# Three entries of a schedule moved: early weight loads, a layer's conversion, one group's row gathers

## The chip, the cores and the metric

The kernel runs on one core of a Trainium2 chip. The metric is the device time of one execution in microseconds (us). Before the change the median of three runs is 801.74 us (800.7 to 805.22).

## What is computed

Three layers follow each other, all in float32 (cut from the reference):

```python
# 1. attention, B, H, S, D = 4, 8, 576, 64
scores = q @ k.T / sqrt(D);  cum = cumsum(max(s, 0))
scores = where(causal, -1e9, scores + min(-(cum_i - cum_j), 0))
x = softmax(scores) @ v                      # -> x: 2304 tokens x 512
# 2. mixture of experts: each token goes to one of 8 experts, D 512, F 1024
e = argmax(x @ w_gate);  gate = softmax(x @ w_gate)[e]
x = gate * (max(x @ w1[e], 0) @ w2[e])
# 3. dense layer, 512 -> 768 -> 512
h = max(x @ m1, x @ m2, x @ m3)              # elementwise maximum of three products
out = h @ w_out
```

The weights of layer 3 arrive as 64-bit words and are turned into float32 on the chip (the "conversion" below).

## The kernel before

**Attention.** The 32 heads are worked in 16 pairs, 4 pairs to a batch. A pair loads k, q, v (`nk`, `nq`, `nv`) and its bias rows `bl` (two DMAs of 528 KB, L218). POOL writes the causal mask into `bl` (L269, L274, L280). PE makes scores (L308, L328), DVE adds the bias and takes the row minimum of the negated scores (L314, L335), ACT takes the exponential (L321, and L343 for the last rows, once to a pair), PE transposes the result (L374), ACT and DVE copy it out of PSUM (L416, L414), PE multiplies by v (L426). While a pair is scored, the pair before it is transposed and multiplied. The expert choice of a batch (L488 to L557) runs beside the pairs after it.

**Experts.** Tokens are gathered by expert into groups of up to 336 rows (`gather`, L926, an indirect DMA on POOL's queue; one buffer of three windows to a group, two buffers), transposed on PE (L932), split into a high and a low float32r half on ACT and DVE (L944, L948) and multiplied in three matmuls (L953). Group 0 takes tokens of the first three batches and starts before attention ends; group 1 is the first full group that waits for the last batch.

**Weight ring.** Expert weights come in pieces of 512 KB: `w_load` (L689, an SP DMA into `wr0` to `wr2`, later also `xr0`, `xr1`), `w_hi` (ACT rounds the piece to its high half, listed as L192) and `w_lo` (DVE subtracts, L697). The first three pieces, `n < R0` (L722), belong to group 0 and are handled during attention. They take their times from five numbers in line 80: `w_hi` of piece n at slot `WE1 + WES * n`, that is 80, 126 and 172, and its load `WE0` slots from there.

**Conversion.** `decode` (L764) takes one of 24 chunks of the dense layer's weights through a load on ACT's queue (`dr`, 512 KB, L735), one ACT operation (L739), six DVE operations (L743 to L759) and a store on ACT's queue (L762). Inside a chunk the ACT operation is due `D0` = 5 us after the load and the store `DST` = 13 us after it.

**What sets the order.** Every step is put into one list with a due slot (`at`, L202; a slot is 0.456 us, a pair lasts `IT` = 25 slots). The list is sorted by slot and emitted (`run_events`, L1103), so the slot fixes only where an instruction stands in its own engine's queue. When it runs is decided by semaphores: a slot starts nothing, and an engine takes its instructions strictly in that order. `TX` is the slot at which the attention's buffers are given up, `TM` the planned start of group 1's matmuls, 11.2 us later in plan time, and `TOV` lies near the end of the last group.

Of the kernel before, what the change touches and what calls it, by code (L numbers as in the profile page):

```python
# [12 lines left out]
I32 = mybir.dt.int32  # L13
# [19 lines left out]
NEARLY = 1  # L33
# [38 lines left out]
LD0, SPL, VT = 3, 9, 10  # L72
WLF = 12
ORD = (3, 1, 2, 0)
D0, DST = 5, 13

WRB, R0, R1, XR, XQ = 3, 3, 2, 2, 1
WHI = "A"
WLO = "V"
WE0, WE1, WES, WEL, WEH = -23, 80, 46, 3, "A"  # L80
WHE, WLE = "A", "V"
SLOT = 0.456
ES, TMS = 5.0, 2
# [15 lines left out]
def emit(nc, tc, qt, kt, v, s, wg, w1, w2, m64, out, dbg=None):  # L99
    V, A, G, T, SP = nc.vector, nc.scalar, nc.gpsimd, nc.tensor, nc.sync  # L100
# [101 lines left out]
    def at(slot, fn, *args):  # L202
        heapq.heappush(evq, (slot, next(seqno), fn, args))
# [424 lines left out]
    TX = max(e[0] for e in evq) + 1  # L628
    cap = [c for e, bs, c in GROUPS]
    TM = max(TX + 13, TA + (ES + NEARLY * 21.2) / SLOT) + TMS  # L630

    def atm(us, fn, *args):
        at(TM + us / SLOT, fn, *args)
# [34 lines left out]
    def pt(g, i):  # L668

        x, k = step[g]  # L670
        us = SL[x] / 8 * i + sum(cost[o] for o in STEPS[x][:k]) / 8 + (GAP12 if i >= 4 else 0)
        return S0[x] + us / SLOT

    TOV = pt(NG - 1, 4) + OVT / SLOT
# [89 lines left out]
    def decode(u, src, dst, n):  # L764
        z = {}
        atm(u, dec_load, z, src, n)
        for x, f in ((D0, dec_abs), (D0 + 1, dec_1), (D0 + 2, dec_2), (D0 + 3, dec_3), (D0 + 4, dec_4)):
            atm(u + x, f, z, n)
        atm(u + DST, dec_st, z, dst, n)


    for n in range(24):
        dst = w32 if n < 18 else wo32
        i, x = divmod(n if n < 18 else n - 18, 2)
        decode((TX - TM) * SLOT + 1 + ((TOV - TX) * SLOT - 4 - DST) / 23 * n, m64[n].bitcast(I32), dst[i, :, 512 * x:512 * x + 512], 512)


    gi = cp.tile([P, NG * NWIN], I32, name="gi")
# [124 lines left out]
    XG1 = max(TR2, TA) + 0.2  # L903
# [102 lines left out]
    gfree = [0.0, 0.0]  # L1006
    for x, gs in enumerate(STEPS):

        span = (S0[x] - 1.3 / SLOT) - max(S0[x] - 9 / SLOT, max([last.get("x", -1e9)] + [last.get("xs", -1e9)]) + 0.3 / SLOT,
                                          TX + 7 if x >= NEARLY else -1e9)  # L1010
        if x == 0:
            span = 1.2 / SLOT
        st_ = min(1.7 / SLOT, max(0.3 / SLOT, span / (4 * len(gs))))
        m = 0
        for g in gs:
            L = cost[g]
            t0 = S0[x] - 1.3 / SLOT - st_ * (4 * len(gs) - m)
            gfree.sort()
            if g == 0:
                at(XG0, gather, g)  # L1020
            else:
                at(max(gfree[0] + 0.01, XG1 if x < NEARLY else TX + 0.2, t0 - 60 / SLOT), gather, g)
                gfree[0] = t0 + st_ * 3 + 0.02
            for kk in range(4):
                t = t0 + st_ * kk
                at(t, xtr, g, kk)
                at(t + 0.3 / SLOT, xhi, g, kk)
                if not small(g):
                    at(t + 0.8 / SLOT, xlo, g, kk)
            m += 4  # L1030
            for f in range(8):
                t = pt(g, f // 2) + (f % 2) * L / 16 / SLOT
                at(t, mm1, g, f)
                at(t + (L / 16 + 0.1) / SLOT, h_hi, g, f)
                if not small(g):
                    at(t + (L / 16 + 0.5) / SLOT, h_lo, g, f)
            last["xs" if small(g) else "x"] = t + L / 16 / SLOT
            for d_ in range(4):
                t = pt(g, 4 + d_)
                at(t, mm2, g, d_)  # L1040
                at(t + (L / 8 + 0.1) / SLOT, y_ev, g, d_)
# [208 lines left out]
```

## Time and profile before

| | us |
|---|---|
| median of three runs | 801.74 |
| lowest, highest | 800.7, 805.22 |
| the profiled execution | 801.6 |
| span of its trace (first to last instruction) | 799.9 |

The trace is of the profiled execution: 1.7 us of its time lie outside the span. From 0 to about 223 us attention runs, with group 0's first matmuls in its last part, then the experts until about 489 us, then the dense layer. A share over the whole span mixes these three; what one step costs is read from its own stretch. In the timelines a value in square brackets is the time for which that engine sat idle before the row, and behind the arrow stands what released it. "SPq" and "ACTq" rows are DMA issues; their duration is the issue, not the transfer.

### The profile page before, as it was taken

Reading aid. Unit: us, or ns where it says so; the run is one execution under the profiler, and the core shown is the slowest. Engines: PE = TensorE matmul, PEld = TensorE weight load, DVE = VectorE, ACT = ScalarE, POOL = GpSimd, SP = SyncE. Lnnn points to the kernel's source line nnn. Section 1 sums busy time; section 2 is a strip of 40 time slices with the busy share of each in tenths; the row PEclk is TensorE's granted clock in tenths of the full one; section 3 lists DMA queues with packets and bytes.
Section 4 is the critical chain, followed back from the end, with each engine's and each line's share of the span. In section 5 each row is a group of like instructions: output and inputs, shape, how many; then the busy total and the mean of one; then the engine's idle time right before and its main releaser. Section 6 shows DMA issues by size and latency. Waiting matters only on the chain. (4 is left out here: it accounts for less than half of the span.)

```text
span 799.9 us, 12890 instructions
## 1 busy us (share of the span) xinstructions
PE 763.0 (95%) x4782; PEld 685.6 (86%) x4782; DVE 436.9 (55%) x1142; ACT 335.4 (42%) x771; POOL 110.8 (14%) x226
## 2 busy tenths in 40 slices
PE   7988999999879999999999999999999999999996
PEld 4755666666679988999999999989989899899995
DVE  6655777677668768889888755422312212222120
ACT  5755666666546443455445545221211211212111
POOL 4332233334130110101200000010010000100001
PEclk9999999999999999999999999999999999999999
DMA  6866968767376687877685535100010000100001
GB/s 187 208 163 168 257 156 246 187 174 238 95 273 229 216 292 255 298 255 265 216 256 196 202 131 152 58 27 14 1 40 1 23 18 1 40 1 14 26 1 40
DMA packets 34876, 112.43 MB, mean 141 GB/s; under 512 B 4793, under 2 KB 4875, under 8 KB 32891
## 3 DMA queue, kind: packets, MB, share of 16 engines
q1 hardware_dynamic: 24107, 81.66, 34.3%
q10 hardware_dynamic: 7456, 18.89, 6.8%
q0 software_dynamic: 3248, 11.03, 3.9%
q8 instruction: 39, 0.64, 0.3%
q14 instruction: 26, 0.21, 0.1%
HBM read 94.97 MB, written 16.60 MB: 139 GB/s over the span
## 5 line engine op out<-in xcount | busy, mean ns | idle before, releaser
L1146 DVE TENSOR_TENSOR mA<-ps_a,mA 128x384 f32<-128x384 f32 x72 | 40.2, 558 | 181.4 <-PE ps_a L953 181.4
L953 PE MATMUL ps_a<-yc,wq 128*128 128x384 f32 x720 | 129.1, 339 | 0.0
L953 PEld LDWEIGHTS ps_a<-yc,wq 128*128 128x128 f32 x720 | 127.4, 188 | 0.4
L953 PE MATMUL ps_c<-h,wq 128*128 128x336 f32 (+1 forms) x672 | 106.3, 316 | 3.1 <-ACTq L870 1.5
L953 PEld LDWEIGHTS ps_c<-h,wq 128*128 128x128 f32 x672 | 101.8, 192 | 3.9 <-ACTq L870 1.8
L953 PE MATMUL ps_a<-yc,wm 128*128 128x384 f32 x576 | 103.7, 339 | 0.0
L953 PE MATMUL ps_a<-xT,wq 128*128 128x336 f32 (+1 forms) x648 | 101.0, 313 | 1.9 <-ACT hs L972 1.6
L953 PEld LDWEIGHTS ps_a<-yc,wm 128*128 128x128 f32 x576 | 101.9, 188 | 0.0
L953 PEld LDWEIGHTS ps_a<-xT,wq 128*128 128x128 f32 x648 | 96.5, 188 | 2.6 <-ACT hs L972 1.8
L953 PE MATMUL ps_c<-wm,g 128*128 128x512 f32 x324 | 76.9, 396 | 0.0
L321 ACT ACTIVATE P<-ns,mn 128x512 f32<-128x512 f32 (+3 forms) x128 | 70.7, 559 | 12.8 <-DVE mn L314 12.8
L1150 ACT ACTIVATE g<-mA 128x384 fp32r<-128x384 f32 x36 | 18.9, 526 | 135.7 <-DVE mA L1146 135.7
L953 PEld LDWEIGHTS ps_c<-wm,g 128*128 128x128 f32 x324 | 60.9, 188 | 14.4
L1169 POOL DMA_INDIRECT out<-o,midi x18 | 17.6, 976 | 378.5 <-ACT o L1165 374.4
L314 DVE CUSTOM_DVE_ANT_0 ns<-ps_a,bl 128x512 f32<-128x512 f32 (+3 forms) x128 | 57.3, 488 | 21.3 <-ACT P L321 11.8
L697 DVE TENSOR_TENSOR wq<-wr,wq 128x1024 fp32r<-128x1024 f32 x44 | 53.6, 1221 | 13.5 <-ACT wq L192 13.0
L426 PE MATMUL ps_c<-ptT,nv 128*64 128x320 f32 (+4 forms) x448 | 51.4, 367 | 5.2 <-DVE ptT L414 5.2
L426 PEld LDWEIGHTS ps_c<-ptT,nv 128*64 128x64 f32 x448 | 29.8, 138 | 31.0 <-DVE ptT L414 12.6
L192 ACT ACTIVATE wq<-wr 128x1024 fp32r<-128x1024 f32 x44 | 46.3, 1055 | 22.4 <-DMA wr<-in_w 22.4
L374 PE MATMUL ps_b<-idf,P 128*128 128x128 f32 x320 | 47.4, 287 | 5.5 <-ACT ptT L416 3.9
L308 PE MATMUL ps_a<-nk,nq 64*128 64x512 f32 (+3 forms) x256 | 48.3, 477 | 2.9 <-DVE mn L314 1.7
L374 PEld LDWEIGHTS ps_b<-idf,P 128*128 128x128 f32 x320 | 35.1, 143 | 15.1 <-ACT ptT L416 9.1
(221 smaller groups left out, 955.5 us busy)
## 6 DMA issues: line engine op xcount, KB each, us to landing
wr<-in_w SPq DMA_DIRECT2D x49, 512.0 KB
bl<-cumd SPq DMA_DIRECT2D x30, 528.0 KB
dr<-in_m ACTq DMA_DIRECT2D x24, 512.0 KB
xr<-in_w SPq DMA_DIRECT2D x23, 512.0 KB
nq<-in_qt SPq DMA_DIRECT2D x16, 352.0 KB
nv<-in_v SPq DMA_DIRECT2D x16, 320.0 KB
nk<-in_kt SPq DMA_DIRECT2D x16, 288.0 KB
xd<-xr SPq DMA_DIRECT2D x4, 1152.0 KB
```

Of the source, the lines that this page charges most:

```text
L192: A.activation(o, x, AF.Copy)
L308: T.matmul(d["sp", i, g][:, :w], d["q"][r, 128 * i:128 * i + 128], d["k"][r, :w], start=True, stop=True)
L314: V.tensor_tensor_reduce(out=ns[:, :w], in0=d.pop(("sp", i, g))[:, :w], in1=d["bl"][:, 1024 * g + BOFF[i]:1024 * g + BOFF[i] + w], scale=- ...
L321: A.activation(pp, d.pop(("ns", i, g))[:, :w], AF.Exp, bias=d["mn"][:, c:c + 1], scale=-1.0, accum_out=ssum[b][:, i, h + g:h + g + 1])
L374: T.transpose(pt[:, c:c + 128], (d["P", "t"] if g == "t" else d["P", g, i])[:, k0:k0 + 128], idf)
L426: T.matmul(po[64 * g:64 * g + 64, qa - c0:c1 - c0], d["v"][:, g, j], d["pt"][:, g, POFF[j] + qa - 128 * j:POFF[j] + c1 - 128 * j], start=( ...
L697: (V if eng == "V" else G).tensor_tensor(t[:, 1], raws.pop(key), t[:, 0].bitcast(F32), ALU.subtract)
L953: T.matmul(ps_, w_(zw), x_(zx), start=(first and n == 0), stop=(last and n == 2))
L1146: V.tensor_tensor(m, pm[:, :CH], m, ALU.max)
L1150: A.activation(t[:, 0], h2[c, f, "m"], AF.Copy)
L1169: G.indirect_dma_start(out, bass.IndirectOffsetOnAxis(ap=midi[:, n:n + 1].bitcast(U32), axis=0), h2.pop((c, x, "s")), None)
```

## The change

Three entries of the schedule get other slots; no operation is added or removed.

```diff
-D0, DST = 5, 13
+DS0, D0, DST = -2, 5, 13
...
-WE0, WE1, WES, WEL, WEH = -23, 80, 46, 3, "A"
+WE0, WE1, WES, WEL, WEH = -45, 80, 46, 3, "A"
...
     for n in range(24):
         dst = w32 if n < 18 else wo32
         i, x = divmod(n if n < 18 else n - 18, 2)
-        decode((TX - TM) * SLOT + 1 + ((TOV - TX) * SLOT - 4 - DST) / 23 * n, m64[n].bitcast(I32), dst[i, :, 512 * x:512 * x + 512], 512)
+        decode(DS0 + ((TOV - TM) * SLOT - DS0 - 3 - DST) / 23 * n, m64[n].bitcast(I32), dst[i, :, 512 * x:512 * x + 512], 512)
...
             if g == 0:
                 at(XG0, gather, g)
             else:
-                at(max(gfree[0] + 0.01, XG1 if x < NEARLY else TX + 0.2, t0 - 60 / SLOT), gather, g)
+                at(max(gfree[0] + 0.01, XG1 if x < NEARLY else TX + 0.2 if x == NEARLY else TM + 4 / SLOT, t0 - 60 / SLOT), gather, g)
```

`WE0`: the loads of the three early pieces are due 45 slots ahead of their `w_hi` instead of 23; `w_hi` and `w_lo` keep their slots. The conversion's first load is due 2.0 us before `TM` instead of 10.2 us before it, the last chunk keeps its place, and the chunks are 7.92 us apart instead of 8.28. The gathers of groups 2 and 3, due at `TX` + 0.2 slots and 3.0 us before `TM`, are both due 4 us after `TM`.

The SP queue around the first early piece, before. `wr0` is the piece; `nk`, `nq`, `nv` and `bl` are a pair's loads, and the `bl` behind the piece belong to the fifth pair:

```order
L213 DMA nk_354<-in_kt 128x576
L213 DMA nq_356<-in_qt 128x704
L218 DMA bl_466<-cumd_63 64x2112 x2
L222 DMA nv_500<-in_v 128x640
L213 DMA nk_502<-in_kt 128x576
L213 DMA nq_504<-in_qt 128x704
L689 DMA wr0_530<-in_w1 128x1024
L218 DMA bl_629<-cumd_63 64x2112 x2
L222 DMA nv_663<-in_v 128x640
```

And after:

```order
L213 DMA nk_354<-in_kt 128x576
L213 DMA nq_356<-in_qt 128x704
L689 DMA wr0_394<-in_w1 128x1024
L218 DMA bl_468<-cumd_63 64x2112 x2
L222 DMA nv_502<-in_v 128x640
L213 DMA nk_504<-in_kt 128x576
L213 DMA nq_506<-in_qt 128x704
L218 DMA bl_629<-cumd_63 64x2112 x2
L222 DMA nv_663<-in_v 128x640
```

The piece moved up past four rows, from in front of the fifth pair's `bl` to in front of the fourth pair's. The second piece moves in the same way, from in front of the seventh pair's `bl` to in front of the sixth's; the third goes from behind the eighth pair's `bl` to behind the seventh's.

POOL's queue at the end of attention, after. `xw` with the first number is group 1's buffer, with the second group 2's, with the third group 3's:

```order
L434 MEMSET oT_2975 128x64
L926 DMA xw_3277<-xd_64,gi_166 128x576 x2
L926 DMA xw_3277<-xd_64,gi_166 80x576
L926 DMA xw_3471<-xd_64,gi_166 128x576 x2
L926 DMA xw_3471<-xd_64,gi_166 80x576
L926 DMA xw_3475<-xd_64,gi_166 128x576
```

Here nothing moved: before, the same rows stand in the same order with the same waits, and only the buffers' numbers differ. The three gathers of group 2 wait for no semaphore in either kernel.

ACT's queue at the same place, before. `dr` is a chunk's raw load, `dc` its working tile, `wq` and `xq` are weight pieces, `yE` is group 0's output and `xT` group 1's input:

```order
L192 ACTIVATE xq0_3271<-wr0_3171 128x1024
L735 DMA dr_3288<-in_m64 128x1024
L997 ACTIVATE yE0_3322<-ps_c_3238 128x256
L192 ACTIVATE wq1_3324<-wr1_3224 128x1024
L944 ACTIVATE xT0_3330<-ps_b_3326 128x336
L944 ACTIVATE xT1_3365<-ps_b_3336 128x336
L997 ACTIVATE yE0_3322<-ps_c_3297 128x256
L192 ACTIVATE wq0_3368<-xr0_3273 128x1024
L739 ACTIVATE dc_3371<-dr_3288 128x512
L944 ACTIVATE xT2_3378<-ps_b_3373 128x336
```

And after:

```order
L192 ACTIVATE xq0_3271<-wr0_3171 128x1024
L997 ACTIVATE yE0_3316<-ps_c_3238 128x256
L192 ACTIVATE wq1_3318<-wr1_3224 128x1024
L944 ACTIVATE xT0_3324<-ps_b_3320 128x336
L944 ACTIVATE xT1_3359<-ps_b_3330 128x336
L997 ACTIVATE yE0_3316<-ps_c_3291 128x256
L192 ACTIVATE wq0_3362<-xr0_3273 128x1024
L944 ACTIVATE xT2_3370<-ps_b_3365 128x336
L997 ACTIVATE yE0_3316<-ps_c_3334 128x256
L192 ACTIVATE wq1_3401<-xr1_3275 128x1024
L944 ACTIVATE xT3_3407<-ps_b_3403 128x336
L735 DMA dr_3411<-in_m64 128x1024
```

The first `dr` load moved down past the four `xT` rows, and the first `dc` operation has left this stretch. It now stands some five rows below its load, among the `h` rows of group 1.

## Rows read from the trace of the kernel before

**Rows 1.** Page, part 1: busy time, share of the span, instructions of each engine

```profile
PE 763.0 (95%) x4782; PEld 685.6 (86%) x4782; DVE 436.9 (55%) x1142; ACT 335.4 (42%) x771; POOL 110.8 (14%) x226
```

**Rows 2.** Stretches: busy us (instructions) of each engine, granted clock, DMA share, GB/s

```profile
40.00:80.00 40.00, 33.36 (x219) 23.39 (x220) 23.35 (x85) 23.58 (x70) 11.26 (x24) 0.91 0.64 166
49.10:52.50 3.40, 3.40 (x16) 2.44 (x16) 2.53 (x11) 2.90 (x11) 1.15 (x4) 0.50 0.01 3
73.00:76.40 3.40, 3.40 (x16) 2.99 (x14) 3.37 (x13) 2.47 (x8) 0.86 (x3) 0.50 0.77 160
160.00:200.00 40.00, 38.86 (x295) 27.61 (x295) 30.39 (x127) 27.35 (x88) 14.23 (x29) 1.00 0.73 205
250.00:480.00 230.00, 223.07 (x1501) 220.92 (x1500) 184.31 (x365) 112.21 (x199) 16.64 (x15) 1.00 0.69 233
```

**Rows 3.** Timeline of ACT: start us, us, operation, idle before and its releaser

```profile
39.35 0.77 ACT L343 ACTIVATE Pt<-nst,mn 128x576 f32<-128x576 f32 x1
...
44.03 1.06 ACT L192 ACTIVATE wq<-wr 128x1024 fp32r<-128x1024 f32 x1 [2.85 <-DMA wr<-in_w]
...
55.75 0.77 ACT L343 ACTIVATE Pt<-nst,mn 128x576 f32<-128x576 f32 x1
...
66.89 0.77 ACT L343 ACTIVATE Pt<-nst,mn 128x576 f32<-128x576 f32 x1
...
71.13 1.06 ACT L192 ACTIVATE wq<-wr 128x1024 fp32r<-128x1024 f32 x1 [3.38 <-DMA wr<-in_w]
...
84.06 0.77 ACT L343 ACTIVATE Pt<-nst,mn 128x576 f32<-128x576 f32 x1
...
96.51 1.05 ACT L192 ACTIVATE wq<-wr 128x1024 fp32r<-128x1024 f32 x1
97.45 0.77 ACT L343 ACTIVATE Pt<-nst,mn 128x576 f32<-128x576 f32 x1
...
109.60 0.77 ACT L343 ACTIVATE Pt<-nst,mn 128x576 f32<-128x576 f32 x1
...
120.73 0.77 ACT L343 ACTIVATE Pt<-nst,mn 128x576 f32<-128x576 f32 x1
...
132.44 0.77 ACT L343 ACTIVATE Pt<-nst,mn 128x576 f32<-128x576 f32 x1
...
144.89 0.77 ACT L343 ACTIVATE Pt<-nst,mn 128x576 f32<-128x576 f32 x1
```

**Rows 4.** Timeline of PE, where the second stall ends

```profile
72.72 1.39 PE L374 MATMUL ps_b<-idf,P 128*128 128x128 f32 x6 [3.70 <-ACT ptT L416]
```

**Rows 5.** Timeline of SP, its DMA issues from 26 to 39 us

```profile
26.99 1.10 SPq L218 DMA_DIRECT2D bl<-cumd  x2
...
37.61 0.42 SPq L689 DMA_DIRECT2D wr<-in_w  x1
38.14 1.09 SPq L218 DMA_DIRECT2D bl<-cumd  x2
```

**Rows 6.** Timeline of POOL, masks of the fourth and fifth pair

```profile
37.13 0.64 POOL L269 TENSOR_SCALAR_AFFINE_SELECT bl<-bl 128x512 f32<-128x512 f32 x1 [4.50 <-DMA bl<-cumd]
...
49.12 0.64 POOL L269 TENSOR_SCALAR_AFFINE_SELECT bl<-bl 128x512 f32<-128x512 f32 x1 [2.28 <-DMA bl<-cumd]
```

**Rows 7.** Timeline of DVE, first scores of the fourth pair

```profile
41.17 0.69 DVE L314 CUSTOM_DVE_ANT_0 ns<-ps_a,bl 128x512 f32<-128x512 f32 x1 [0.58 <-PE ps_a L308]
```

**Rows 8.** Waits of PE from 205 to 530 us: total, times, longest

```profile
PE ps_b L932 <- DMA xw<-xd,gi: 2.9, 2, 1.5
```

**Rows 9.** Timeline of POOL, first gather of group 1

```profile
228.56 1.98 POOL L926 DMA_INDIRECT xw<-xd,gi  x1 [20.92 <-DVE r_os L552]
```

**Rows 10.** DMA queues from 231 to 234 us: packets, MB, share of 16 engines

```profile
q10 hardware_dynamic: 142, 0.52, 44.5%
```

**Rows 11.** The same from 234 to 240 us

```profile
q1 hardware_dynamic: 303, 1.11, 50.8%
q0 software_dynamic: 289, 1.06, 50.7%
```

**Rows 12.** Waits of ACT from 205 to 530 us

```profile
ACT dc L739 <- DMA dr<-in_m: 6.1, 5, 1.9
```

## The prediction

> **What bounds the kernel now.** I read the page first. PE is busy for 763.0 of 799.9 us [rows 1], so at most 37 us can be won by filling its gaps, and the question is whose gaps the change touches. The stretches come next. From 250 to 480 us PE is busy for 223.07 of 230 us [rows 2]: the expert stage is bound by PE, and a transfer that moves there is worth something only where PE waits for it. From 40 to 80 us it is busy for 33.36 of 40 us at a mean granted clock of 0.91, against 38.86 of 40 us at 1.00 from 160 to 200 us [rows 2]. So attention has a weak place early on.
>
> The timeline of ACT shows what it is. L343 runs once for each pair of heads, so the distance between two of its rows is what a pair costs. Undisturbed pairs cost 11.13 us (109.60 to 120.73), 11.71 (to 132.44) and 12.45 (to 144.89), by their place in the batch. Two pairs cost far more: 39.35 to 55.75 is 16.40 us and 66.89 to 84.06 is 17.17 us [rows 3]. In each stands an L192, the rounding of an early weight piece, for which ACT sat idle for 2.85 and 3.38 us until the piece's DMA landed [rows 3]. All exponentials and copies behind it in ACT's queue stood still as well, and after the second PE had been idle for 3.70 us, released by ACT's copy [rows 4]. In the stretches 49.10 to 52.50 and 73.00 to 76.40 us, each behind one of these stalls, the granted clock is 0.50, the lower level of 1.2 GHz [rows 2]. Work that follows TensorE's clock takes up to 1.7 us longer in each.
>
> **Part 1, the early pieces.** No operation is added or removed; three DMAs of 512 KB move up in SP's queue. The first now stands where the fourth pair's `bl` was issued, at 26.99 us, and not at 37.61 [rows 5]. From its issue to the end of ACT's wait it took 44.03 - 37.61 = 6.42 us [rows 3, 5]. So it is there at about 33.4 us. ACT reaches the L192 at 44.03 - 2.85 = 41.18 us, so the wait goes with 7.8 us to spare. The second piece gains one pair as well, and loses its wait in the same way.
>
> What is left of the two long pairs: the rounding itself stays. The third piece shows what that costs, since its L192 at 96.51 did not wait: the pair 84.06 to 97.45 takes 13.39 us where its counterpart takes 12.45, so 0.94 us [rows 3]. The second long pair corresponds to 11.71, which makes 12.65, and it saves 17.17 - 12.65 = 4.52 us. The first lies in the first batch, beside no earlier batch's expert choice; the pair behind it takes 11.14 us (55.75 to 66.89), so I take 11.13 + 0.94 = 12.07 and a saving of 4.33 us. Together 8.85 us. As bounds: the two waits alone are 6.23 us, and the whole excess over 11.13 and 11.71, with the rounding hidden, is 5.27 + 5.46 = 10.73 us. A wait plus a full 1.7 us for the clock would be 4.55 and 5.08 us, which brackets the same size.
>
> What the pieces push back: `bl` now stands behind a piece. Without one in front it took from its issue at 26.99 to the mask's start at 37.13, 10.14 us; with one in front from 38.14 to 49.12, 10.98 us [rows 5, 6]. So 0.84 us are added. The mask takes 0.64 us, and DVE first needs it at 41.17 [rows 6, 7], so it may start as late as 40.53: 3.40 us are spare, and I price this at nothing. The third piece only goes ahead of an `nv`, which is first read a pair later. Nothing in SP's queue gets a new wait, and the queue behind the old places becomes shorter by the same 512 KB.
>
> **Part 2, the gathers of groups 2 and 3.** In POOL's queue no row changes its place, and no row between group 1's gathers and group 2's could hold them back. They run as before, directly behind group 1's, and this entry is worth 0.
>
> **Part 3, the conversion.** The first `dr` load leaves the time in which PE waits for group 1's rows, 2.9 us in two waits [rows 8], after a gather that POOL starts at 228.56 [rows 9]. From 231 to 234 us that load used 44.5% of the sixteen DMA engines, which is 1.34 us of all of them [rows 10]. Behind it, from 234 to 240 us, the gathers' queue q0 has 50.7% and SP's weight queue q1 50.8% [rows 11]. If all later traffic moves up, the last row arrives 1.34 us sooner; if SP's pieces take the freed time, nothing is won. The new first chunk is due where the second stood, so nothing new enters this window and I see no loss. I take the middle, 0.67 us.
>
> The Trainium skill ("DMA: Bandwidth & Descriptors", section "Queues, rings and completion order") says that each DMA engine takes the queues that have work in turn. The even split of 50.7 to 50.8 agrees. By that rule the freed turns go to SP's pieces, part 3 is worth 0, and the sum is 792.8 instead of the one below.
>
> In the expert stage the 24 chunks stay, 7.92 us apart instead of 8.28, and each begins up to 8.2 us later. ACT waited for a `dr` load five times, 6.1 us in all and 1.9 us at most [rows 12]. Other chunks will now meet a busy time; I take 0, with one longest wait, 1.9 us, either way. All later stages follow from the one before and start earlier by what attention gains.
>
> **Sum.** 801.6 (the profiled execution) - 8.85 - 0 - 0.67 + 0 = 792.1 us. That execution is 0.14 us under the median of the runs, 801.74, which I neglect. With all bounds together: 801.6 - 10.73 - 1.34 - 1.9 = 787.6 and 801.6 - 6.23 + 1.9 = 797.3.
>
> **Rivals.** *Only the waits go.* Behind the piece something else is just as late, a PSUM bank or DVE's part of the rounding, and the pairs shrink by 6.23 us alone: 795.4. For it speaks that pairs are chains over four engines; against it that undisturbed pairs run in 11.13 to 12.45 us.
>
> *The mask becomes the wait.* If the piece held up `bl` for its whole 6.42 us, the mask would be 3.02 us too late in two pairs: 792.1 + 6.0 = 798.1. It decides from a delay of 3.40 us on; 0.84 was seen. The Trainium skill (same page and section) gives the reason for it, that descriptors of one queue are consumed in ring order on each DMA engine. By the page's 435 GB/s a piece would add an estimated 1.2 us, less than what is spare.
>
> *The pieces stay late.* Were ACT's wait not the transfer but something that SP meets in any place of its queue, only part 3 would be left: 800.9. The 7.8 us of room speak against it.
>
> *More goes than I count.* The gathers' wait of 2.9 us vanishes whole, and the conversion saves one longest wait: 801.6 - 8.85 - 2.9 - 1.9 = 788.0.
>
> *Slower: the conversion blocks ACT.* Each chunk has an ACT operation that waits for its `dr` load while evictions that PE needs queue behind it. A late one costs 6.1 / 5 = 1.22 us. With the new spacing 17 of 24 could be late instead of five, and if PE follows each time: 792.1 + 12 x 1.22 = 806.7. It turns into a loss from 8 more late chunks on (9.5 / 1.22). Against it: the load goes down before PE's busiest stretch and not up, and PE has only 6.93 us of gaps there from all causes [rows 2].
>
> **How the numbers follow.** The forecast has 0.57 (its own range 790 to 794.5), more than I count 0.14, only the waits 0.14, the mask 0.06, pieces still late 0.04, slower 0.05. A measurement of this kernel can tell about 0.5%, 4.0 us, from no change. The first three are faster by more than that, 0.85; the mask and the late pieces lie within, 0.10; slower 0.05. The range of 787.5 to 797.0 holds the first three.
>
> **What would show it.** After: no idle before the first two L192 rows; L343 distances of about 12.1 and 12.6 us in place of 16.40 and 17.17; a granted clock of 1.00 from 40 to 80 us; the mask of the fourth pair 0.8 us later after its `bl`'s issue and no wait of L314 for POOL; group 2's gathers directly behind group 1's; the wait at L932 down by 0.7 us. Attention should end about 8.9 us earlier, and the rest keep its length. I am wrong if the long pairs stay above 14 us, if DVE waits for the mask, or if the stretch from the first gather of group 1 to the end changes by more than 3 us.

## The result and the profile after

The changed kernel takes 794.4 us (median of 4 runs, 793.69 to 796.26), the kernel before 802.06 us beside it (4 runs, 800.7 to 805.22). The ratio is 0.989, with a 95% interval of 0.9855 to 0.9925. The forecast of 792.1 us lay 2.3 us too low, inside its range. The profiled execution of the changed kernel is the slowest of its four, 796.26 us with a span of 794.4 us.

The page's row of PE answers to [rows 1]: the busy time is 1.4 us less, the span 5.5 us less. The gain lies in PE's gaps.

```profile
PE 761.6 (96%) x4782; PEld 685.4 (86%) x4782; DVE 436.2 (55%) x1142; ACT 335.8 (42%) x771; POOL 108.3 (14%) x226
```

The stretches, in the columns of [rows 2]. From 40 to 80 us PE is busy for 38.04 us in place of 33.36, and the granted clock is 1.00 in place of 0.91. From 250 to 480 us it is 221.96 in place of 223.07: here the expert stage lost a little. The last row is a stretch that the kernel before did not have in this place, 6.83 us at 0.50, the level of 1.2 GHz.

```profile
40.00:80.00 40.00, 38.04 (x283) 26.32 (x279) 29.90 (x113) 28.70 (x86) 13.70 (x28) 1.00 0.81 226
250.00:480.00 230.00, 221.96 (x1477) 219.97 (x1476) 180.50 (x359) 109.90 (x195) 15.42 (x15) 0.99 0.70 231
309.78:316.61 6.83, 5.97 (x21) 5.98 (x22) 5.67 (x15) 2.60 (x5) 0.00 (x0) 0.50 0.89 303
```

ACT's timeline answers to [rows 3]. Both L192 rows have lost the bracket with their idle time: the pieces are there. The distances 38.44 to 50.46 and 61.59 to 74.45 are 12.02 and 12.85 us where 16.40 and 17.17 stood, so 4.39 and 4.32 us are gone.

```profile
38.44 0.77 ACT L343 ACTIVATE Pt<-nst,mn 128x576 f32<-128x576 f32 x1
...
40.15 1.06 ACT L192 ACTIVATE wq<-wr 128x1024 fp32r<-128x1024 f32 x1
...
50.46 0.77 ACT L343 ACTIVATE Pt<-nst,mn 128x576 f32<-128x576 f32 x1
...
61.59 0.77 ACT L343 ACTIVATE Pt<-nst,mn 128x576 f32<-128x576 f32 x1
62.35 1.04 ACT L192 ACTIVATE wq<-wr 128x1024 fp32r<-128x1024 f32 x1
...
74.45 0.77 ACT L343 ACTIVATE Pt<-nst,mn 128x576 f32<-128x576 f32 x1
```

Three timelines show the mask of the fourth pair. First SP's issues [rows 5]: the piece `wr` now stands ahead of `bl`.

```profile
25.75 0.43 SPq L689 DMA_DIRECT2D wr<-in_w  x1
26.29 2.42 SPq L218 DMA_DIRECT2D bl<-cumd  x2
```

Then POOL's mask [rows 6] and, in the second fence, DVE's first scores [rows 7]. From the issue of `bl` to the mask it is 38.25 - 26.29 = 11.96 us, 1.82 more than the 10.14 of before. The mask ends at 38.88, DVE starts at 40.27 and waits for PE, so 1.4 us of the 3.4 are left.

```profile
38.25 0.63 POOL L269 TENSOR_SCALAR_AFFINE_SELECT bl<-bl 128x512 f32<-128x512 f32 x1 [6.54 <-DMA bl<-cumd]
```

```profile
40.27 0.69 DVE L314 CUSTOM_DVE_ANT_0 ns<-ps_a,bl 128x512 f32<-128x512 f32 x1 [0.59 <-PE ps_a L308]
```

The lists of waits from 205 to 530 us (total, times, longest), of PE and of ACT, answer to [rows 8] and [rows 12]. A wait of PE for L999 has grown to 2.8 us in one place. ACT's waits for `dr` have doubled, 12.3 us after 6.1.

```profile
PE ps_b L932 <- DMA xw<-xd,gi: 3.5, 3, 1.8
PE ps_c L953 <- ACT yT L999: 2.8, 1, 2.8
```

```profile
ACT wq L192 <- DMA wr<-in_w: 16.8, 6, 5.2
ACT dc L739 <- DMA dr<-in_m: 12.3, 9, 3.8
```

For the gathered rows the list shows 3.5 us after 2.9, but the list of before leaves out one of three waits, for which the profile names no releaser ("issue"). PE's timeline has all three, first of before and then of after: 1.53 + 1.01 + 1.36 = 3.90 us became 0.63 + 1.77 + 1.08 = 3.48, so 0.4 us are gone.

```profile
236.48 0.30 PE L932 MATMUL ps_b<-idf,xw 128*128 128x128 f32 x1 [1.53 <-DMA xw<-xd,gi]
237.79 0.33 PE L932 MATMUL ps_b<-idf,xw 128*128 128x128 f32 x1 [1.01 <-issue]
239.48 0.58 PE L932 MATMUL ps_b<-idf,xw 80*128 80x80 f32 x4 [1.36 <-DMA xw<-xd,gi]
```

```profile
226.85 0.30 PE L932 MATMUL ps_b<-idf,xw 128*128 128x128 f32 x1 [0.63 <-DMA xw<-xd,gi]
228.92 0.33 PE L932 MATMUL ps_b<-idf,xw 128*128 128x128 f32 x1 [1.77 <-DMA xw<-xd,gi]
230.33 0.58 PE L932 MATMUL ps_b<-idf,xw 80*128 80x80 f32 x4 [1.08 <-DMA xw<-xd,gi]
```

The place where PE waits for L999, in ACT's timeline. The load of 512 KB for `dr` is issued between two roundings L192 that wait for weight pieces. The second waits 5.20 us, a third stands behind it, and only then comes L999, which PE needs. PE's rows below, of after and then of before, show what follows: 2.84 us idle in place of 1.45, and then 24 matmuls in 6.65 us, which take 3.96 us at full clock.

```profile
300.58 1.06 ACT L192 ACTIVATE wq<-wr 128x1024 fp32r<-128x1024 f32 x1 [3.17 <-DMA wr<-in_w]
300.76 0.33 ACTq L735 DMA_DIRECT2D dr<-in_m  x1
...
307.49 1.06 ACT L192 ACTIVATE wq<-wr 128x1024 fp32r<-128x1024 f32 x1 [5.20 <-DMA wr<-in_w]
309.19 1.06 ACT L192 ACTIVATE wq<-wr 128x1024 fp32r<-128x1024 f32 x1 [0.64 <-DMA wr<-in_w]
...
310.15 0.43 ACT L999 ACTIVATE yT<-ps_c 128x336 f32 x1
```

```profile
310.63 6.65 PE L953 MATMUL ps_c<-h,wq 128*128 128x336 f32 x24 [2.84 <-ACT yT L999]
```

```profile
319.10 3.96 PE L953 MATMUL ps_c<-h,wq 128*128 128x336 f32 x24 [1.45 <-ACT yT L999]
```

The account of the two profiled executions, from start times in both timelines: the first L343 comes 0.90 us earlier (16.54 for 17.44), the two pairs save 8.71, and with one later pair, 0.20 shorter, attention ends 9.81 us earlier. A stretch of half clock at 200.55 us, which run 4 of the same kernel does not have, takes 1.06 back; the gathers give 0.38. From there to the end 3.70 us are lost again, and the place just shown accounts for them: PE waits 1.39 us longer there and its next 24 matmuls take 2.69 us longer, together 4.08. The end comes 5.43 us earlier. From group 1's first gather to the end it is 574.6 us in place of 571.3.

### The profile page after: what moved, and what is told of

It reads as the page before. It is cut to its first block, busy times and chain, and to the rows that moved or that the text cites. A ratio compares the mean times of both kernels' runs of the same rounds, so it can differ in the third digit from the quotient of the medians.

```text
span 794.4 us, 12902 instructions
## 1 busy us (share of the span) xinstructions
PE 761.6 (96%) x4782; PEld 685.4 (86%) x4782; DVE 436.2 (55%) x1142; ACT 335.8 (42%) x771; POOL 108.3 (14%) x226
## 5 line engine op out<-in xcount | busy, mean ns | idle before, releaser
L953 PE MATMUL ps_c<-h,wq 128*128 128x336 f32 (+1 forms) x672 | 108.8, 321 | 4.4 <-ACT yT L999 2.8
L953 PEld LDWEIGHTS ps_c<-h,wq 128*128 128x128 f32 x672 | 104.6, 196 | 4.8 <-ACT yT L999 3.0
L1169 POOL DMA_INDIRECT out<-o,midi x18 | 17.5, 973 | 379.4 <-ACT o L1165 375.2
L697 DVE TENSOR_TENSOR wq<-wr,wq 128x1024 fp32r<-128x1024 f32 x44 | 53.8, 1225 | 9.3 <-ACT wq L192 8.7
L192 ACT ACTIVATE wq<-wr 128x1024 fp32r<-128x1024 f32 x44 | 46.4, 1056 | 16.8 <-DMA wr<-in_w 16.8
L926 POOL DMA_INDIRECT xw<-xd,gi x22 | 23.0, 1047 | 172.3 <-PE ps_b L932 145.7
```

The lines of the kernel that those rows point to most:

```text
L192: A.activation(o, x, AF.Copy)
L697: (V if eng == "V" else G).tensor_tensor(t[:, 1], raws.pop(key), t[:, 0].bitcast(F32), ALU.subtract)
L926: G.indirect_dma_start(xw[n][x][0:k], None, rows, bass.IndirectOffsetOnAxis(ap=src[0:k, c:c + 1].bitcast(U32), axis=0))
L953: T.matmul(ps_, w_(zw), x_(zx), start=(first and n == 0), stop=(last and n == 2))
L1169: G.indirect_dma_start(out, bass.IndirectOffsetOnAxis(ap=midi[:, n:n + 1].bitcast(U32), axis=0), h2.pop((c, x, "s")), None)
```

## The experiments

Theory A: the pieces win all of it in attention, and the moved conversion gives some back in the expert stage. Rival B: the expert stage gives back whatever arrives early, the conversion has no part in it. Rival C: the pieces win little. The first four runs shared runs of the kernel before (803.21 us), the next four as well (804.25), and the last four (803.8). Gains in us below are the ratio's distance from 1 times that median.

**1. The pieces alone**

```diff
-WE0, WE1, WES, WEL, WEH = -23, 80, 46, 3, "A"
+WE0, WE1, WES, WEL, WEH = -45, 80, 46, 3, "A"
```

> The kernel before with the three early pieces 45 slots ahead and nothing else. Theory A (the pieces win about 8.7 us in attention, and the moved conversion gives some back in the expert stage, where ACT's waits for dr grew from 6.1 to 12.3 us and PE got a 2.84 us stall): L343 distances 12.0 and 12.85 as in the changed kernel, no stall near 310 us over 2 us, and 791 to 793 us, 1 to 3 us under the changed kernel's 794.4. Rival B (the give-back comes from arriving earlier, whatever the conversion does): the stall is there as well, and 794.4 us. Rival C (the pieces win little, the conversion's move the rest): over 797 us.

793.15 us, ratio 0.9867 (0.9836 to 0.9898): 10.7 us gained. The pieces carry the whole gain, and C falls. In its profile the expert stage gave nothing back: 6.8 us were gained at group 3's first gather and 8.1 at the end, and PE's wait for L999 is 1.54 us with no half clock behind it. So arriving early costs nothing by itself, and B falls too, by the profile: the times of runs 1 and 4 have intervals that overlap. The run showed something else as well, in POOL's and DVE's timelines:

```profile
41.95 0.63 POOL L269 TENSOR_SCALAR_AFFINE_SELECT bl<-bl 128x512 f32<-128x512 f32 x1 [9.43 <-DMA bl<-cumd]
```

```profile
42.62 0.69 DVE L314 CUSTOM_DVE_ANT_0 ns<-ps_a,bl 128x512 f32<-128x512 f32 x1 [2.15 <-POOL bl L269]
```

`bl` was issued at 27.16, so the mask came 14.79 us later, and DVE waited 2.15 us for it. The pair took 13.48 us in place of 12.02. The rival in which the mask becomes the wait did happen, in this execution and in one pair.

**2. The conversion alone**

```diff
-        decode((TX - TM) * SLOT + 1 + ((TOV - TX) * SLOT - 4 - DST) / 23 * n, ...
+        decode(DS0 + ((TOV - TM) * SLOT - DS0 - 3 - DST) / 23 * n, ...
```

> The kernel before with the conversion's new start and spacing and nothing else. Theory A: the wait at L932 for group 1's rows falls by about 0.4 us, and the expert stage loses 1 to 3 us: 803 to 805 us. Rival B: 801.5 to 802.5 us. Rival C: 797 us or less. L343 distances as before, 16.4 and 17.2 us, in all three.

805.39 us, ratio 1.0025 (1.0002 to 1.0048): 2.0 us lost. ACT's waits for `dr` are as in the changed kernel:

```profile
ACT dc L739 <- DMA dr<-in_m: 13.6, 10, 4.0
```

But the profile does not show the loss in the expert stage. Its execution, 803.27 us, is one of the fastest of the twelve; PE's wait for L999 is 1.61 us there, without half clock, and from group 1's first gather to the end it is 570.8 us, against 571.3 before. The long pairs took 16.2 and 19.6 us, the second 2.4 more than expected. Where the 2.0 us of the times arise stays open in this run; run 10 tests the same entry again.

**3. The gathers' entry alone**

```diff
-                at(max(gfree[0] + 0.01, XG1 if x < NEARLY else TX + 0.2, t0 - 60 / SLOT), gather, g)
+                at(max(gfree[0] + 0.01, XG1 if x < NEARLY else TX + 0.2 if x == NEARLY else TM + 4 / SLOT, t0 - 60 / SLOT), gather, g)
```

> The kernel before with the later slot of the gathers of groups 2 and 3 and nothing else. No row of POOL's queue moves, so all theories expect 802 us within 1 us, and group 2's first gather about 1.3 us behind group 1's last, as before. Were the slot to matter, those gathers would start some 10 us later.

803.25 us, ratio 0.9999 (0.9972 to 1.0026). Group 2's gathers follow group 1's as before. The entry changes nothing that can be measured.

**4. The changed kernel again**

> The changed kernel once more, beside the parts. 794.4 us within 1 us. If its stall near 310 us and the half-clock stretch behind it are the same as in the first profile, they belong to the kernel; if they are gone, to that execution.

794.4 us, ratio 0.9888 (0.9854 to 0.9922), 9.0 us gained. The three parts add up to it, within their intervals: 10.7 - 2.0 + 0.1 = 8.8. PE's wait for L999 is there again, 3.65 us, and so is the half clock behind it, 6.83 us from 307.53 on. It belongs to the kernel and not to one execution.

**5. All three pieces ahead of one `bl`**

```diff
-            ld = hi + WE0
+            ld = WE1 + WE0
```

> The changed kernel, but all three early pieces are issued in front of the fourth pair's mask load `bl`, 1.5 MB in place of 0.5 MB. Before the change that load took 10.14 us from its issue to the mask's start without a piece ahead of it, and about 2 us more in the changed kernel with one. Theory A (pieces delay `bl` because it stands behind them in the same queue, about 2 us each): three cost 6 us, the mask comes 2 to 3 us too late for DVE, DVE waits at L314 for the mask, the fourth pair takes 14 to 15 us in place of 12.02, the sixth pair stays at 12.6 to 12.9, total 796 to 797.5. Rival (the delay of `bl` has another cause, such as what else the DMA engines carry at that time): the mask starts within 1 us of where it does in the changed kernel, the pair stays near 12.0 and the total at 794.4.

796.95 us, ratio 0.9908 (0.9892 to 0.9924). In SP's and POOL's timelines the mask comes 43.93 - 27.37 = 16.56 us after the issue; DVE's row shows who pays:

```profile
27.37 1.77 SPq L218 DMA_DIRECT2D bl<-cumd  x2
```

```profile
43.93 0.63 POOL L269 TENSOR_SCALAR_AFFINE_SELECT bl<-bl 128x512 f32<-128x512 f32 x1 [12.14 <-DMA bl<-cumd]
```

```profile
44.60 0.69 DVE L314 CUSTOM_DVE_ANT_0 ns<-ps_a,bl 128x512 f32<-128x512 f32 x1 [4.86 <-POOL bl L269]
```

Without a piece in front the fourth pair's `bl` takes 9.95 to 11.87 us from issue to mask (eight profiles: before and runs 2, 3 and 8 to 12), so three pieces cost 4.7 to 6.6 us here, 1.6 to 2.2 each. One piece does not stand clear of that spread: it is 11.96 us in after, but 14.79, 9.87, 10.86 and 11.01 in runs 1, 4, 6 and 7. The pair took 18.31 us and not the 14 to 15 expected: a stretch of half clock from 47.15 us on, 6.83 us long, followed DVE's wait. The Trainium skill ("DMA: Bandwidth & Descriptors", section "Queues, rings and completion order") says that the descriptors of one queue are consumed in ring order on each engine; the trace agrees for three pieces, 16.56 us against at most 11.87 without.

**6. The roundings in another place**

```diff
-WE0, WE1, WES, WEL, WEH = -45, 80, 46, 3, "A"
+WE0, WE1, WES, WEL, WEH = -60, 95, 50, 3, "A"
```

> The changed kernel, with the three early roundings on ACT (L192, 1.06 us each) moved in their pair from the middle of the exponentials to just ahead of the last L435, where ACT has idle time; the pieces are issued where they are now. The prediction kept 0.94 us for each rounding in the two long pairs, and the bound was that it hides. If the rounding is hidden there: the two pairs take 11.1 to 11.7 us in place of 12.02 and 12.85, the third 12.4 in place of 13.40, and the total is 2 to 3 us lower, 791.5 to 792.5. If the exponentials are not what the pair waits for, or the copy behind the rounding is late in its turn: the distances stay within 0.3 us, and the total at 794.4.

791.4 us, ratio 0.9834 (0.981 to 0.9859), against 0.9888 for the changed kernel (run 4). By the new numbers the third piece is issued ahead of the eighth pair's `bl` and no longer directly behind the seventh's; the first two stay where they were. ACT's timeline shows the rounding just ahead of L435, which waits for PE all the same:

```profile
47.36 1.06 ACT L192 ACTIVATE wq<-wr 128x1024 fp32r<-128x1024 f32 x1
49.16 0.44 ACT L435 ACTIVATE oT<-ps_c 128x320 f32<-128x320 f32 x1 [0.74 <-PE ps_c L426]
49.49 0.77 ACT L343 ACTIVATE Pt<-nst,mn 128x576 f32<-128x576 f32 x1
```

The pairs with a rounding take 11.13, 11.70 and 12.45 us, exactly what undisturbed ones take; the third had 13.40. So all that was left over in these pairs was the rounding, 0.89, 1.15 and 0.95 us, and it hides.

**7. The conversion's loads further ahead of their use**

```diff
-DS0, D0, DST = -2, 5, 13
+DS0, D0, DST = -2, 9, 17
```

> The changed kernel, with each chunk of the conversion's first operation on ACT four planned slots (about 4 us) further behind its load; where the loads begin is as in the changed kernel, their spacing about 0.2 us less. Theory A (the moved conversion costs about 2 us because ACT's operation on `dc` waits for its `dr` load, and the evictions behind it hold up PE): ACT's waits for `dr` fall from 12 to 16 us to under 5 us, the PE stall of about 3 us near 307 to 310 us with its half clock behind it goes, total 791 to 792.5. Rival (what costs is the transfers' traffic in the expert stage, since the wait for the weight piece at L192 also holds ACT there): the waits for `dr` fall, but the wait at L192 for `wr` and PE's stall near 307 to 310 us remain, total 794 to 795.

793.25 us, ratio 0.9852 (0.9833 to 0.9872). No wait of ACT for `dr` is left, but ACT's list and PE's timeline show that the stall is still there:

```profile
ACT wq L192 <- DMA wr<-in_w: 13.2, 5, 5.5
```

```profile
309.73 5.49 PE L953 MATMUL ps_c<-h,wq 128*128 128x336 f32 x24 [2.90 <-ACT yT L999]
```

My reason, ACT's waits for `dr`, falls for this place: what holds L999 there is the rounding that waits for its weight piece. Whether the waits for `dr` cost something elsewhere is not settled: the time lies 0.0036 of the ratio below run 4, with intervals that overlap.

**8. Pieces behind `bl`, roundings moved, the old conversion**

```diff
-WE0, WE1, WES, WEL, WEH = -23, 80, 46, 3, "A"
+WE0, WE1, WES, WEL, WEH = -45, 95, 50, 3, "A"
```

> The early pieces alone moved, with the conversion and the gathers as before the change; the pieces are issued directly behind the `bl` of the fourth, sixth and eighth pair and not in front of it, and the roundings stand ahead of the last L435 of their pair. If `bl` was late in the version with the pieces alone because a piece stood ahead of it: `bl` takes 10 to 10.5 us from issue to mask again, DVE doesn't wait for the mask, and with the roundings hidden the long pairs take 11.1 to 11.8 us. Theory A's sum: 793.15 (pieces alone) - 1.4 (the mask wait) - 2 to 3 (roundings) = 789 to 790. If the roundings don't hide: 791.7. If the pieces, issued later, are late again: L192 waits for `wr`, 795 or more.

788.62 us, ratio 0.9813 (0.9797 to 0.9828), just below the sum. The sum does not hold the start-up, which is 1.0 us shorter in this profile than in that of run 1 (below), so part of the agreement is luck. The mask starts 36.02 - 26.07 = 9.95 us after the issue of `bl` (11.44 in run 12, the same version), and DVE does not wait for it:

```profile
36.02 0.63 POOL L269 TENSOR_SCALAR_AFFINE_SELECT bl<-bl 128x512 f32<-128x512 f32 x1 [4.17 <-DMA bl<-cumd]
```

The pieces are still early enough, no early L192 waits. This version is faster than both kernels.

**9. No conversion while weight pieces are late** (version 8 with another timing)

```diff
-        decode((TX - TM) * SLOT + 1 + ((TOV - TX) * SLOT - 4 - DST) / 23 * n, ...
+        at_ = -2 + 7.92 * n if n < 4 else 74 + ((TOV - TM) * SLOT - 3 - DST - 74) / 19 * (n - 4)
+        decode(at_, ...
```

> The version with the pieces behind `bl`, the roundings ahead of the last L435 and the gathers as before (788.6 us), with another timing of the conversion: four chunks from the changed kernel's start on, then none between about 267 and 315 us, the stretch in which ACT waits for weight pieces at L192, and the other twenty 5.6 us apart behind it. Theory D (the stall of PE near 307 us comes from a `dr` load of 512 KB that shares the DMA engines with the four weight pieces due there): ACT's waits at L192 for `wr`, 14 us in all, fall to 8 us or less, no PE wait for L999 over 1 us remains there, no half clock between 290 and 320 us, and 787 to 788 us unless the denser chunks behind it cost waits for `dr` that PE feels. Rival (the pieces are late since SP issues them late, behind waits for buffers, whatever else moves): the waits at L192 stay at 12 to 15 us, PE waits 1 to 2 us for L999, and the time is 788.6 or above.

793.87 us, ratio 0.9873 (0.9851 to 0.9895), slower than version 8. ACT's waits at L192 stayed, 14.2 us, so in sum they do not come from `dr` loads beside the pieces, as the rival said. The chunks behind the pause came too densely: ACT waited for their stores, 17.5 us. From group 3's first gather to the first matmul of the dense layer it is 246.0 us, against 238.3 in run 12; that the stores are the reason is likely but not tested alone.

```profile
ACT dc L739 <- DMA w<-dc: 17.5, 8, 3.4
ACT wq L192 <- DMA wr<-in_w: 14.2, 6, 4.2
```

```profile
305.38 3.96 PE L954 MATMUL ps_c<-h,wq 128*128 128x336 f32 x24 [1.46 <-ACT yT L1000]
```

At the disputed place (line numbers are one higher in this version) PE waits 1.46 us, as the rival expected and theory D did not, and keeps its clock, as theory D expected.

**10. Version 8 with the new conversion**

> The version of 788.6 us with the changed kernel's conversion and nothing else. If the moved conversion costs by itself, whatever the start of the expert stage: 2 to 3 us more than the same version with the old one, 790.5 to 791.5, with a PE wait for L999 of 1.8 to 3.6 us and a half clock near 300 to 310 us, and ACT's waits for `dr` at 11 to 16 us. If the loss in the changed kernel came from where its attention happened to end: within 1 us of the version with the old conversion.

791.87 us, ratio 0.9856 (0.9834 to 0.9879), beside 789.65 for version 8 in the same batch (run 12): 2.2 us lost by the conversion alone, by medians of five runs each, with intervals that overlap in part. From group 3's first gather to the dense layer it is 242.1 us in the profile, against 238.3 in run 12. Its pattern of ACT is that of the changed kernel, and PE waits and slows down again:

```profile
297.25 1.06 ACT L192 ACTIVATE wq<-wr 128x1024 fp32r<-128x1024 f32 x1 [2.18 <-DMA wr<-in_w]
298.03 0.33 ACTq L735 DMA_DIRECT2D dr<-in_m  x1
304.87 1.06 ACT L192 ACTIVATE wq<-wr 128x1024 fp32r<-128x1024 f32 x1 [4.78 <-DMA wr<-in_w]
```

```profile
307.83 5.35 PE L953 MATMUL ps_c<-h,wq 128*128 128x336 f32 x24 [2.62 <-ACT yT L999]
```

Where the old conversion stands, as in version 8, the load is issued only at the second of these L192, not before it:

```profile
297.07 1.06 ACT L192 ACTIVATE wq<-wr 128x1024 fp32r<-128x1024 f32 x1 [4.34 <-DMA wr<-in_w]
302.67 1.06 ACT L192 ACTIVATE wq<-wr 128x1024 fp32r<-128x1024 f32 x1 [3.48 <-DMA wr<-in_w]
302.68 0.33 ACTq L735 DMA_DIRECT2D dr<-in_m  x1
```

The two L192 are 5.5 to 6.0 us apart in the seven profiles without a load between them (before, runs 1, 3, 8, 9, 11, 12), and 6.8 to 8.8 us in six of the seven with one (after, runs 4, 5, 6, 7, 10; in run 2 it is 6.15). The six have the half clock behind it, the others not.

Two parts of this distance grew. The first is the transfer of the second piece: from SP's issue to the second L192 it is 3.13 to 3.69 us without the load and 3.80 to 5.67 with it. SP's rows, of this run and then of run 8, stand 5.27 and 3.26 us ahead of the L192 at 304.87 and 302.67:

```profile
299.60 0.33 SPq L689 DMA_DIRECT2D wr<-in_w  x1
```

```profile
299.41 0.33 SPq L689 DMA_DIRECT2D wr<-in_w  x1
```

One `dr` load was 1.34 us of the sixteen DMA engines [rows 10], which is of that size. The second part is the issue itself, 2.3 us behind the first L192 in eleven of the fourteen profiles and 2.9 to 3.1 in runs 4, 5 and 6. It follows the end of DVE's L697, which subtracts the first piece. In these three DVE comes to it late, from two operations of a moved chunk (L743, L745), in run 4 with the L192 done at 298.24 and SP's issue at 300.31:

```profile
299.06 1.22 DVE L697 TENSOR_TENSOR wq<-wr,wq 128x1024 fp32r<-128x1024 f32 x1
```

No run moved this one chunk by itself, so both links are read from fourteen profiles and not tested alone.

This run and run 6 differ in whether the pieces stand behind or in front of `bl` (and in the gathers' entry, worth nothing): 0.9856 and 0.9834, with intervals that overlap. That the place behind `bl` wins anything is not shown.

**11. Group 2's gathers really held back** (version 8, and POOL first copies one number of group 1's last rows)

```diff
+    hold = cp.tile([1, 1], F32, name="hold")
     def gather(n):
 ...
+        if n == 2:
+            G.tensor_copy(hold, xw[1][2][0:1, 0:1])
```

> The version of 788.6 us, in which POOL copies one number of group 1's last gathered rows before it starts group 2's gathers, so that these really begin behind the landing of group 1's, which the change's entry alone did not bring about. If the gathers of group 2 take DMA time from group 1's rows: PE's waits at L932 for `xw`, 4.4 us in three, fall to 2 us or less, and the total by 1.5 to 3 us, to 786 to 787. If group 1's rows are late for another reason (start of the gather, the weight pieces of SP): the waits at L932 stay within 1 us, 788.6. If group 2's rows become late themselves, a new wait at L932 near 240 us: 789 or more.

784.06 us, ratio 0.9754 (0.9737 to 0.9772), the fastest of all, but not for the reason tested. The gathers were held: group 2's first starts 11.3 us behind group 1's first, in place of 4.8 in runs 8 and 12. PE's wait for the rows is what it was in run 12, 4.0 us (L932 is L936 here):

```profile
PE ps_b L936 <- DMA xw<-xd,gi: 3.9, 3, 1.6
```

When the last stage began, at 476.5 us, this execution was 1.6 us behind run 8, and it ended 3.0 us ahead of it. The time is won in the last stage, whose instructions the edit doesn't touch. PE's groups from 520 to 760 us, first of run 12 and then of run 11:

```profile
L953 PE MATMUL ps_a<-yc,wq 128*128 128x384 f32 x600 | 107.6, 339 | 0.0
```

```profile
L957 PE MATMUL ps_a<-yc,wq 128*128 128x384 f32 x600 | 105.7, 336 | 0.0
```

The mean distance of two such matmuls is 173.4 ns here, and 176.7 ns in before, after, run 8 and run 12, with the granted clock at 1.00 in all. The edit adds a tile of four bytes among the constants and one instruction on POOL; which of the two does it, by the place of the tiles or of the code behind them, was not tried.

**12. Version 8 again**

> The version with the pieces behind `bl`, the roundings moved, the conversion and the gathers as before, a second time beside the three variants of it: 788 to 789.5 us, 14.5 to 15.5 us under the kernel before, no PE wait for L999 over 1.5 us, a single stretch of half clock before the end, near 227 us.

789.65 us, ratio 0.9833 (0.9814 to 0.9852), a little above what was expected; run 8 had 0.9813. Against the expectation, a second stretch of half clock, at 197.69 us, which run 8 did not have, took 1.0 us.

## Why the prediction was right, and where not

**The bound.** Right: ACT's waits for the early pieces, and PE's gaps and clock behind them, were what could be won. Attention gained 9.81 us, 0.90 of them by the start-up (below), and the granted clock is 1.00 from 40 to 80 us.

**The two pairs.** Right, mechanism and size: 4.39 us for 4.33 and 4.32 for 4.52, together 8.71 of 8.85. That the rest was the rounding, 0.94 us a pair, is shown by run 6, where it hides and the pairs fall to their undisturbed lengths; the upper bound of 10.73 us was within reach. But the size is that of two executions: in the profiles of runs 2 and 3, where the pieces stand as before, the two pairs take 35.8 and 34.3 us together, and in before 33.6. That fits the larger gain of the times, 10.7 us in run 1 (8.2 to 13.2 by its interval).

**The mask.** Right that DVE does not wait in the changed kernel. The price of 0.84 us was read from one pair of rows [rows 5, 6], and one pair cannot give it: in the fourth pair one piece added 1.82 us in after, and 1.0 on the mean (11.70 us in the five profiles with one in front, 10.70 in the eight without), while the eight differ by 1.9 among themselves. By the 435 GB/s of the Trainium skill (the page named in run 5, section "Specifications") the estimate was 1.2 us; three pieces gave 1.6 to 2.2 each, and the measurement decides. The rival that I gave 0.06 was nearer than that: of 3.4 us, 1.3 to 2.7 are left in after and runs 4, 6 and 7, and in run 1 nothing.

**The gathers.** Right: 0 forecast, and 0.9999 for the entry alone.

**The conversion at the gathers' wait.** Right in sign, and near in size: 0.4 us for the 0.67 forecast. Group 1's first transpose came 7.03 us after the first gather in place of 7.92, but the second then waited longer, 1.77 us for 1.01. The 2.9 us that I started from [rows 8] left that second wait out; the three make 3.90. Over all profiles they make 3.26 to 3.79 us with the new start (after, runs 2, 4 to 7, 9, 10) and 3.85 to 4.37 with the old one (before, runs 1, 3, 8, 11, 12).

**The conversion in the expert stage.** Here the prediction failed: "I take 0, with one longest wait, 1.9 us, either way". It is a loss of 3.7 us in the profiled execution, and of 2.2 us (run 10 beside run 12) and 2.0 us (run 2, whose profile does not show it there) by the times, so the bound of 1.9 was too small as well. One of my own signs of being wrong came true: the stretch from group 1's first gather to the end was to change by no more than 3 us, and it grew by 3.3 (in run 4 by 2.5). I looked for the loss in ACT's operations that wait for `dr`. They did double, as the slower rival had it, but run 7 took all of them away and PE's stall stayed. The order that I had before me showed the loads moving among the other rows of ACT, and I followed only the first of them; I did not ask what else is in transfer where each of the 24 lands. One falls among the weight pieces that ACT is waiting for already, and beside it a piece takes 3.80 to 5.67 us from issue to rounding in place of 3.13 to 3.69; in three profiles the chunk's work on DVE also delays the issue (run 10). This term has the size of the 2.3 us between forecast and result. The forecast's range held the result because it was wide enough for one term of this size, not because the term was foreseen.

**The start-up.** It was not in the sum. The first L343 comes at 17.43 to 17.44 us in before and runs 1 and 3, and at 16.4 to 16.5 us in all other profiles, although nothing that stands ahead of it was changed in any. In the three, PE's four matmuls L328 near 14.5 us take 2.29 us, in the others 1.28 to 1.41, at the same granted clock of 1.00. The cause stays open. In the profiled execution these 0.90 us nearly offset the 1.06 us lost to the half clock at 200.55 us; neither was forecast, so this is luck.

## What to carry to other kernels

A wait of an in-order engine for a transfer is worth its idle time and what the clock loses behind it; the length of an undisturbed period next to the disturbed one prices both at once, and here it did so to 2% between two executions. A load that is moved ahead can delay what it passes in its queue, and one pair of rows does not tell by how much: read it from several executions before you price it. And when a periodic stream is moved, follow every one of its transfers to the place where it lands, above all where an engine already waits for other data.

## What was not expected of the hardware

- PE's matmuls of 384 columns in the last stage came 176.7 ns apart in one version and 173.4 in another (run 11), at the same granted clock, with instructions that were not edited. Over some 1,300 of them it is over 4 us, more than most edits here. In the start-up, too, PE was slower in three profiles at the same granted clock (2.29 us for 1.28 to 1.41); whether it has the same origin is open.
- Short stalls of PE were followed by stretches of 3.41 or 6.83 us at a granted clock of 0.50, and not each time: behind 2.62 us of idle time it was 3.41 us (run 10), behind 2.84 and 3.65 us 6.83 us (after, run 4), and behind 1.46 and 1.61 us none (runs 9 and 2).
